# The last o stage by seven block products, and a new order for the second half of a causal attention and squared-ReLU MLP kernel

## The chip, the cores and the metric

The kernel runs on one core of a Trainium2 chip. The metric is device time in microseconds (us) of one execution; the profiled execution is one of its runs, read instruction by instruction. The engines are named as the profile names them: PE is the matrix engine (PEld its weight loads), DVE the vector engine, ACT the scalar engine, POOL the general engine, SP the engine that only issues DMAs (SPq, ACTq and POOLq are the DMA issues of those engines).

## What is computed

```python
# q, k, v: 4 batches x 12 heads x 448 x 64, float32; w_in 768 x 2048, w_out 2048 x 768
scores = scale * q @ k.T                      # per batch and head, causal mask
attn = softmax(scores)
x = (attn @ v).transpose(0, 2, 1, 3).reshape(1792, 768)
h = np.maximum(x @ w_in, 0.0)
out = (h * h) @ w_out
```

## The kernel before, in words

**Products.** Every float32 operand of the MLP is split into a high and a low float32r part, and one product of 128 x 128 by 128 x 448 elements is three matmuls: high by high, high by low, low by high. The MLP works in the transposed sense: tiles of h and of the output have features on the partitions and the 448 tokens of one batch along the row.

**Two halves.** The tokens of batches 0 and 1 (the first half) go through plain products (`h_unit`, `o_unit`), while the attention of the other two batches runs between them. The second half, batches 2 and 3, is worked as a 2 x 2 block scheme: x, w_in and w_out are cut in blocks 11, 12, 21, 22, and sums of blocks (s1 to s4 of the weights, t1 to t4 of the left factors) let seven block products do what eight would do. The stages of the second half take the four groups of 512 hidden features in the order `TURNS = (0, 3, 2, 1)`. `h_pair(gr, u)` makes one half of a group's h (21 products of three matmuls), and `o_seven(gr)` multiplies it with w_out and adds to sums in SBUF (`late["sum"]`, tiles sa and sb) after each product: 7 products x 3 column blocks d x 2 halves u x 3 = 126 matmuls.

**The last o stage.** For the last group, gr = 1, `o_last` works without the seven-product scheme: 4 output blocks x 3 column blocks x 4 products x 3 = 144 matmuls. Each of its 12 output tiles lies in one PSUM bank (tiles ps), is added on DVE to its sum (line 269), transposed on DVE (line 1019) and stored by four DMAs (line 1024, issued by SP or ACT). The last tile, block 22 with d = 2, goes through `finish` instead: two adds, four small transposes on PE (line 1046), copies on ACT and DVE (line 1055), and three DMAs (line 1061).

**Weights.** `w_parts` and `o_parts` bring the weight blocks. Blocks 11, 12 and 22 are loaded ready split by SP (line 944 for w_out, from the DRAM tensor wo_split; line 783 for w_in). The sums s1 to s4 come from `added_up`: SP loads two whole blocks (line 718), POOL issues DMAs that add further blocks onto them in SBUF (line 725), ACT or POOL copies (line 735), and `split` makes the high part (line 266 on ACT, line 279 on POOL) and the low part (line 269 on DVE or 273 on POOL). The last o stage before takes four direct loads a half and no `added_up`. A finished weight block lies in one of nine slots of kind "w": eight pieces of the tile wi, and w3. The slot of a block is taken up again once the last matmul that reads it is through.

**The order.** No scheduler runs. Every operation of the plan has a code in the table `PLACES`: sorting by it gives the order of issue, and the code modulo 3 says which of the offered engines does it. Each engine works through its own operations in that order, and semaphores hold an instruction until its operands are there and its buffer is free. Banks and slots are handed out in this order too.

The lines of the profile that the prediction uses: 843, 845, 847 (matmuls of `h_pair`), 969 to 971 (matmuls of both o stages), 266 (any ACT copy or function), 269 (any two-operand DVE operation), 273 (the same on POOL), 279 and 735 (POOL copies).

## Time and profile before

| | |
|---|---|
| median of 3 runs (lowest to highest) | 601.54 us (601.0 to 602.06) |
| the profiled execution, its own time | 601.9 us |
| its span, first to last instruction | 599.8 us |
| outside the span | 2.1 us |
| PE busy | 582.2 us, 97% |
| DVE, ACT, POOL busy | 454.8, 351.7, 274.5 us |
| the chain that ended last: share of PE | 91% |

The page shows one execution. Busy times of an engine overlap with those of others; the chain that ended last tells what the end waited for, step by step back from the last instruction. A matmul's own duration in the trace (0.36 us) is longer than the distance to the next one's start (0.20 us), since matmuls are pipelined: what a matmul costs the engine is that distance.

### The profile page before, as it was taken

The page shows a single profiled execution, that of the slowest core. Times are in us where ns is not written, and L with a number is a line of the kernel's source. Part 1 is how long each engine was busy: PE and PEld are TensorE (multiplying, and loading weights), DVE is VectorE, ACT ScalarE, POOL GpSimd, SP SyncE. Part 2 cuts the span into 40 slices and gives each one's busy share as a digit, 9 for nine tenths or more (in the row PEclk, how much of TensorE's full clock was granted, in tenths as well). Part 3 has the DMA queues.
Part 4 walks back from the last instruction along what each step waited for, and adds up shares of the span by engine and source line. Part 5 has one row for each costly group of instructions (what it writes and reads, how often), then busy time and mean ns, then how long its engine had stood idle before and what let it go on. Part 6 is the DMA issues. An engine that isn't in the chain of part 4 may idle for free.

```text
span 599.8 us, 11359 instructions
## 1 busy us (share of the span) xinstructions
PE 582.2 (97%) x3718; PEld 510.0 (85%) x3718; DVE 454.8 (76%) x1077; ACT 351.7 (59%) x893; POOL 274.5 (46%) x378
## 2 busy tenths in 40 slices
PE   3899999999999999999999999999999999999997
PEld 2577778798988998988889889999999999999996
DVE  5999998688966898897798658577638758776674
ACT  3899987776756853767457442247565645633310
POOL 2566652243135352333224453654766566756310
PEclk9899999999999999999999999999999999999999
DMA  8888534999888987995899699867877766773556
GB/s 148 188 174 203 141 65 111 259 275 315 225 249 248 267 221 171 298 288 154 222 294 309 219 294 277 252 195 175 234 159 172 149 142 144 168 174 60 162 97 103
DMA packets 190650, 119.99 MB, mean 200 GB/s; under 512 B 126016, under 2 KB 178560, under 8 KB 190592
## 3 DMA queue, kind: packets, MB, share of 16 engines
q1 hardware_dynamic: 169488, 107.99, 64.4%
q0 software_dynamic: 6912, 9.44, 10.2%
q10 hardware_dynamic: 14192, 1.85, 1.9%
q8 instruction: 29, 0.48, 0.4%
q14 instruction: 29, 0.24, 0.1%
HBM read 80.71 MB, written 38.54 MB: 199 GB/s over the span
## 4 chain that ended last, share of the span: by engine, by line
PE 91%; ACT 3%; DMA 3%; DVE 1%; SPq 1%; issue 0%; POOL 0%; ACTq 0%
PE ps L1081 7%; PE ps L662 7%; PE ps L1083 7%; PE ps L1082 7%; PE ps L464 6%; PE ps L663 6%; PE ps L664 6%; PE ps L847 6%; PE ps L845 6%; PE ps L843 6%; PE ps L971 6%; PE ps L969 6%; PE ps L970 6%; PE ps L422 6%; PE ps L380 5%; ACT bp L397 1%
## 5 line engine op out<-in xcount | busy, mean ns | idle before, releaser
L266 ACT ACTIVATE words<-words 128x384 f32<-128x384 f32 (+3 forms) x128 | 73.6, 596 | 35.1 <-DVE words L269 11.4
L1081 PE MATMUL ps<-wo,g 128*128 128x384 f32 x224 | 77.3, 345 | 0.0
L393 DVE CUSTOM_DVE_ANT_0 ps<-ps,mask 128x64 f32<-128x64 f32 (+6 forms) x168 | 68.0, 444 | 11.1 <-PE ps L380 9.7
L1083 PE MATMUL ps<-wo,g 128*128 128x384 f32 x224 | 75.1, 335 | 0.0
L1082 PE MATMUL ps<-wo,g 128*128 128x384 f32 x224 | 75.1, 335 | 0.0
L397 ACT ACTIVATE ap<-ps,mx 128x256 f32<-128x256 f32 (+6 forms) x126 | 58.8, 479 | 26.4 <-DVE mx L393 25.5
L662 PE MATMUL ps<-x,wi 128*128 128x448 f32 x192 | 73.7, 384 | 0.0
L663 PE MATMUL ps<-x,wi 128*128 128x448 f32 x192 | 70.2, 365 | 0.0
L664 PE MATMUL ps<-x,wi 128*128 128x448 f32 x192 | 70.2, 365 | 0.0
L406 POOL TENSOR_SCALAR ap<-ap,asm 128x256 f32<-128x256 f32 (+6 forms) x80 | 43.0, 555 | 46.1 <-DVE asm L499 20.6
L970 PE MATMUL ps<-g,wi 128*128 128x448 f32 x153 | 56.0, 366 | 0.0
L971 PE MATMUL ps<-g,wi 128*128 128x448 f32 x153 | 56.0, 366 | 0.0
L969 PE MATMUL ps<-g,wi 128*128 128x448 f32 x153 | 56.0, 366 | 0.0
L273 POOL TENSOR_TENSOR wi<-words,wi 128x384 fp32r<-128x384 f32 (+1 forms) x38 | 45.7, 1227 | 21.4 <-ACT wi L266 20.6
L845 PE MATMUL ps<-x,wi 128*128 128x448 f32 x150 | 55.0, 367 | 0.0
L847 PE MATMUL ps<-x,wi 128*128 128x448 f32 x150 | 55.0, 367 | 0.0
L843 PE MATMUL ps<-x,wi 128*128 128x448 f32 x150 | 54.9, 366 | 0.0
L266 ACT ACTIVATE r<-ps 128x448 f32<-128x448 f32 x56 | 30.1, 542 | 35.5 <-PE ps L847 18.1
L269 DVE TENSOR_TENSOR g<-r,g 128x448 fp32r<-128x448 f32 x54 | 37.4, 703 | 11.1 <-ACT g L266 7.0
L266 ACT ACTIVATE r<-r 128x448 f32<-128x448 f32 x58 | 32.9, 574 | 17.8 <-DVE r L269 17.1
L1081 PEld LDWEIGHTS ps<-wo,g 128*128 128x128 f32 x224 | 42.1, 188 | 1.0 <-issue 0.4
L266 ACT ACTIVATE wi<-words 128x384 fp32r<-128x384 f32 (+1 forms) x53 | 28.5, 545 | 24.6 <-PE ps L970 8.5
(158 smaller groups left out, 1470.4 us busy)
## 6 DMA issues: line engine op xcount, KB each, us to landing
words<-in_moe_w_in_dram SPq DMA_DIRECT2D x24, 512.0 KB, 5.5
words<-in_moe_w_out_dram SPq DMA_DIRECT2D x32, 384.0 KB, 3.8
wo_split<-wo SPq DMA_DIRECT2D x26, 384.0 KB, 4.5
wi<-wo_split SPq DMA_DIRECT2D x22, 384.0 KB, 3.6
wo_whole<-words SPq DMA_DIRECT2D x32, 192.0 KB, 3.5
wi_split<-wi SPq DMA_DIRECT2D x24, 256.0 KB, 3.7
v<-in_v_dram SPq DMA_DIRECT2D x24, 192.0 KB, 4.0
wi_whole<-words SPq DMA_DIRECT2D x18, 256.0 KB, 4.0
```

The source lines that it names most:

```text
L266: return (ACT, t_act(n, psum, more), lambda: nc.scalar.activation(dst(), src(), func, **kw))
L662: nc.tensor.matmul(o, w[:, 0], x[:, 0], start=c == 0, stop=False)
L663: nc.tensor.matmul(o, w[:, 0], x[:, 1], start=False, stop=False)
L664: nc.tensor.matmul(o, w[:, 1], x[:, 0], start=False, stop=c == NP - 1)
L845: nc.tensor.matmul(o, w.t[:, 0, c], x[:, 1], start=False, stop=False, skip_group_check=True)
L847: nc.tensor.matmul(o, w.t[:, 1, c], x[:, 0], start=False, stop=c == CB - 1, skip_group_check=True)
L969: nc.tensor.matmul(o, w.t[:, 0, d], g.t[:, 0], start=start, stop=False, skip_group_check=True)
L970: nc.tensor.matmul(o, w.t[:, 0, d], g.t[:, 1], start=False, stop=False, skip_group_check=True)
L971: nc.tensor.matmul(o, w.t[:, 1, d], g.t[:, 0], start=False, stop=stop, skip_group_check=True)
L1081: nc.tensor.matmul(res(), g[:, 0], w[:, 0], start=f == 0, stop=False)
L1082: nc.tensor.matmul(res(), g[:, 0], w[:, 1], start=False, stop=False)
L1083: nc.tensor.matmul(res(), g[:, 1], w[:, 0], start=False, stop=f == GF - 1)
```

## The change

The last o stage goes by seven products too. `o_last` now loops over the column blocks d outermost, and within a d over the seven products of `O_LAST`, which says for each product its bank and the sum that it is added to: 7 x 3 x 2 x 3 = 126 matmuls. The products 11, 12, s1 open a bank; s2 and 12 go on in another product's bank, so that a bank is added to a sum on DVE more than once while it fills. `put_out` holds the transposes and stores, and the last tile, which goes through `finish`, is block 21 with d = 2. The last `h_pair`'s four results are no longer only split: they are combined by three subtractions into t1 to t4 and split like the other groups'. The last group's w_out blocks come by three direct loads a half and by `added_up`. The buffers of x (tiles x_t and x2_) are handed on once the last `h_pair` has read them, as slots of kind "g7" (factors) and "w" (weights). The stages of the end change places: (1,0), (1,1), o of group 2, o of group 1, where before o of group 2 stood between (1,0) and (1,1). Two stores to wo_split fall away.

```diff
+    lent_x = dict(zip(
+        [(key, i) for key in ("11", "21", "t3", "t1", "t2", "t4", "22") for i in range(CB)],
+        plan.lend("g7", [lambda i=i: x7[("11", "21", "t3")[i // CB], i % CB]() for i in range(3 * CB)])
+        + plan.lend("w", [...])))
...
-            if (a % 2, ch) != (0, 1) or gr == TURNS[-1]:
+            if (a % 2, ch) != (0, 1):
...
-    def h_pair(gr, u, W, rank, step, plain):
+    def h_pair(gr, u, W, rank, step):
...
-        if plain:
-            factor("12", "12", True)
-            return rank
         less("11", "12", "11")
         factor("t1", "11", True)
...
+    O_LAST = {"11": ("a", "11"), "12": ("b", "11"), "s2": ("a", "12"), "s1": ("c", "22"),
+              "s3": ("a", "22"), "s4": ("c", "12"), "22": ("a", "21")}
...
-        for m, key in enumerate(("11", "12", "22") if gr != TURNS[-1] else ("11", "12", "21", "22")):
+        for m, key in enumerate(("11", "12", "22")):
...
-            if gr != TURNS[-1]:
-                added_up(rank, CH, source, done, lambda t: t, True)
+            added_up(rank, CH, source, done, lambda t: t, True)
...
-        for k in ("11", "21", "12", "22"):
-            i, j = k
-            for d in range(CB):
-                ps, a = Hold("ps", "os"), o_sum(k, d)
-                rank = o_product(ps, [(W[i + m, u], g7[TURNS[-1], m + j, u]) for m in "12" for u in range(2)],
-                                 d, True, True, rank, step)
-                if (k, d) == ("22", CB - 1):
-                    finish(ps, a, d, rank)
+        bank = {}
+        for d in range(CB):
+            for key, (b, k) in O_LAST.items():
+                begin = key in ("11", "12", "s1")
+                if begin:
+                    bank[b] = Hold("ps", "os")
+                ps, a = bank[b], o_sum(k, d)
+                rank = o_product(ps, [(W[key, u], g7[TURNS[-1], OTHER[key], u]) for u in range(2)],
+                                 d, begin, True, rank, step)
+                if (key, d) == ("22", CB - 1):
+                    finish(ps, k, d, rank)
                     continue
...
+                plan.op(rank, [on_dve(S, a, lambda ps=ps: ps.t[:, :S], a, ALU.add)], [ps], [("sum", k, d)],
+                        drop=[ps] if key in ("12", "22", "s4") else [])
+                if key in ("12", "22", "s3", "s4"):
+                    put_out(k, d, rank)
...
-        stages += [(a, 0) for a in after] + [(gr, None)] + [(a, 1) for a in after]
+        early_pair = after == TURNS[-1:]
+        stages += [(a, 0) for a in after] + [(a, 1) for a in after if early_pair]
+        stages += [(gr, None)] + [(a, 1) for a in after if not early_pair]
...
+            if all(v is None for _, v in stages[n + 1:]):
+                for key, ops in used.items():
+                    over(ops, [lent_x[key, i] for i in range(CB)])
```

The table `PLACES` is another one for the second half. On PE the two programs have the same order up to about 1150 matmuls before the end. 18 matmuls of 448 columns are gone, and nothing else changes in PE's number of instructions. Over the whole program DVE gets 16 two-operand operations of 448 elements more and one of 384 less; ACT gets 28 copies or functions more; POOL gets 16 two-operand operations more, 8 copies less and 8 accumulating DMAs (line 725) more; SP issues 24 direct w_out loads instead of 26, 28 loads of line 718 instead of 24, and 24 stores to wo_split instead of 26.

Where the order differs, at the places that are spoken of below (all line numbers of the program after are some five to fifteen higher; tile names are followed by a buffer number). **SP**, some 165 us before the last matmul: the loads of split blocks of w_out (`wi<-wo_split`) and w_in (`wi<-wi_split`) into slots of wi, before:

```order
L783 DMA wi_91<-wi_split 128x768 [waits DMAHW3_49,PE_49]
L783 DMA wi_91<-wi_split 128x768 [waits DMAHW4_49,PE_49]
L718 DMA words_96<-wi_whole 128x384 [waits DMAHW5_49,DMASW2_49,DVE_49]
L718 DMA words_96<-wi_whole 128x384 [waits DMAHW6_49,DMASW3_49,DVE_49]
L783 DMA wi_91<-wi_split 128x768 [waits DMAHW7_49,DMAHW3_49,PE_49]
L944 DMA wi_91<-wo_split 128x768 [waits DMAHW0_49,PE_49]
L944 DMA wi_91<-wo_split 128x768 [waits DMAHW1_49,DVE_49,PE_49]
L944 DMA w3_4300<-wo_split 128x768 [waits DMAHW2_49,DVE_49,PE_49]
```

and after:

```order
L788 DMA wi_91<-wi_split 128x768 [waits DMAHW4_49,PE_49]
L788 DMA wi_91<-wi_split 128x768 [waits DMAHW5_49,PE_49,Pool_49]
L949 DMA wi_91<-wo_split 128x768 [waits DMAHW6_49,PE_49]
L949 DMA wi_91<-wo_split 128x768 [waits DMAHW7_49,PE_49]
L949 DMA wi_91<-wo_split 128x768 [waits DMAHW6_49,DMAHW0_49,PE_49]
L949 DMA wi_91<-wo_split 128x768 [waits DMAHW1_49,DVE_49,PE_49]
L949 DMA wi_91<-wo_split 128x768 [waits DMAHW4_49,DMAHW2_49,PE_49]
```

The sixth row of after (it waits for DVE too) is the load whose slot is freed on PE by a matmul of line 852, `ps5_118<-x11_90,wi_91`, and which the matmul `ps1_114<-g3_1_4339,wi_91` of line 973 reads 22 rows of PE later; in the program before no slot is refilled in fewer than 28 rows.

**PE**, some 48 us before the end of after, where a bank (ps4) is emptied by ACT between two products; the nearest such place before (ps2, at 558.44 us of the trace):

```order
L847 MATMUL ps2_115<-x2_8_3924,wi_91 128x448
L843 MATMUL ps7_120<-x2_81,wi_91 128x448
L845 MATMUL ps7_120<-x2_81,wi_91 128x448
L847 MATMUL ps7_120<-x2_81,wi_91 128x448
L843 MATMUL ps3_116<-x4_83,wi_91 128x448
L845 MATMUL ps3_116<-x4_83,wi_91 128x448
L847 MATMUL ps3_116<-x4_83,wi_91 128x448
L843 MATMUL ps2_115<-x6_85,wi_91 128x448 [waits Activation_49]
```

and after:

```order
L852 MATMUL ps4_117<-x2_5_3921,wi_91 128x448
L848 MATMUL ps1_114<-x8_87,wi_91 128x448
L850 MATMUL ps1_114<-x8_87,wi_91 128x448
L852 MATMUL ps1_114<-x8_87,wi_91 128x448
L973 MATMUL ps4_117<-g3_95,w3_4342 128x448 [waits Activation_49]
```

Between the matmul that completes the bank and the one that waits for ACT there are six matmuls before and three after.

**DVE**, some 35 us before the end. Before:

```order
L269 TENSOR_TENSOR g2_94<-r2_99,g2_94 128x448
L269 TENSOR_TENSOR g2_94<-r5_102,g2_94 128x448 [waits Activation_49]
L269 TENSOR_TENSOR sb6_4316<-sb6_4316,sa0_3925 128x448
L269 TENSOR_TENSOR g0_92<-f3_0_4301,g0_92 128x448 [waits Activation_49]
L269 TENSOR_TENSOR sb7_4317<-ps1_114,sb7_4317 128x448 [waits PE_49,Pool_49]
L269 TENSOR_TENSOR sb6_4316<-ps5_118,sb6_4316 128x448 [waits DVE_49,PE_49]
L1019 STREAM_TRANSPOSE words_96<-sb6_4316 128x448 [waits DVE_49]
```

and after:

```order
L274 TENSOR_TENSOR sb3_4355<-ps7_120,sb3_4355 128x448 [waits PE_49]
L274 TENSOR_TENSOR x2_0_3916<-r5_102,x2_0_3916 128x448 [waits Activation_49]
L274 TENSOR_TENSOR x2_5_3921<-f3_2_4345,x2_5_3921 128x448 [waits Pool_49]
L274 TENSOR_TENSOR g3_0_4338<-r4_101,g3_0_4338 128x448
L274 TENSOR_TENSOR sb1_4353<-ps3_116,sb1_4353 128x448 [waits PE_49]
L274 TENSOR_TENSOR sb0_4352<-ps4_117,sb0_4352 128x448 [waits DVE_49]
L274 TENSOR_TENSOR sb3_4355<-sb3_4355,sa0_3925 128x448 [waits DVE_49]
```

The last factors (x2 and g tiles that had been x's and g's buffers) are made between adds from PSUM banks of the o stages. Counted in the order, the last 198 matmuls (two stretches of 99) have beside them on DVE 14 two-operand operations on SBUF alone, 36 adds from PSUM and 11 transposes, where before had 13, 21 and 11; and on POOL 18 two-operand operations, where before had 6.

**DVE**, the last rows. Before:

```order
L269 TENSOR_TENSOR sb10_4320<-ps3_116,sb10_4320 128x448 [waits PE_49]
L1019 STREAM_TRANSPOSE words_96<-sb10_4320 128x448 [waits DVE_49]
L269 TENSOR_TENSOR sb11_4321<-ps0_113,sb11_4321 128x192 [waits PE_49,Pool_49]
L269 TENSOR_TENSOR sb11_4321<-ps0_113,sb11_4321 128x256
L1055 COPY words_96<-ps6_119 128x128 [waits DMAHW5_49,DMAHW2_49,DMAHW6_49,DMAHW1_49,PE_49]
```

and after:

```order
L1034 STREAM_TRANSPOSE words_96<-sb11_4363 128x448 [waits DVE_49,Activation_49]
L274 TENSOR_TENSOR sb8_4360<-ps2_115,sb8_4360 128x448 [waits PE_49]
L274 TENSOR_TENSOR sb5_4357<-ps4_117,sb5_4357 128x448 [waits PE_49]
L1034 STREAM_TRANSPOSE words_96<-sb5_4357 128x448 [waits DMAHW6_49,DMAHW5_49,DMAHW7_49,DMAHW0_49,DVE_49]
L274 TENSOR_TENSOR sb8_4360<-ps6_119,sb8_4360 128x256 [waits PE_49,Pool_49]
L274 TENSOR_TENSOR sb8_4360<-ps6_119,sb8_4360 128x192
```

Before, one add and one transpose stand between two tiles' ends; after, the last tile (sb8) is added to twice, with another tile's add and transpose between, and a POOL addition onto it (sb8 with sa2) stands between its two adds. The bank ps2 of its first add is completed nine matmuls before the last one.

## Rows read from the trace of the kernel before

**Rows 1.** The page: busy time, 40 slices, chain.
```profile
span 599.8 us, 11359 instructions
PE 582.2 (97%) x3718; PEld 510.0 (85%) x3718; DVE 454.8 (76%) x1077; ACT 351.7 (59%) x893; POOL 274.5 (46%) x378
...
PE   3899999999999999999999999999999999999997
...
PEclk9899999999999999999999999999999999999999
...
PE 91%; ACT 3%; DMA 3%; DVE 1%; SPq 1%; issue 0%; POOL 0%; ACTq 0%
```
**Rows 2.** Windows of 20 us: busy us (instructions) by engine, clock, DMA share, GB/s.
```profile
360.00:380.00 20.00, 20.00 (x114) 19.79 (x114) 16.80 (x32) 6.39 (x12) 9.86 (x13) 1.00 0.92 277
...
420.00:440.00 20.00, 20.00 (x99) 18.20 (x98) 12.08 (x18) 12.53 (x26) 15.17 (x20) 1.00 0.77 198
...
540.00:560.00 20.00, 20.00 (x99) 18.38 (x99) 14.42 (x23) 7.44 (x16) 10.73 (x14) 1.00 0.32 80
560.00:580.00 20.00, 20.00 (x101) 18.53 (x100) 13.30 (x22) 6.02 (x12) 6.31 (x7) 1.00 0.52 132
580.00:600.00 20.00, 15.44 (x77) 13.63 (x75) 9.85 (x18) 0.38 (x1) 2.27 (x2) 0.93 0.62 105
```
**Rows 3.** PE's waits: line waited for, us in total, times, longest.
```profile
PE ps L380 <- DVE aqt L351: 7.4, 1, 7.4
...
PE ps L1046 <- DVE sb L269: 0.5, 1, 0.5
```
**Rows 4.** Timeline of PE, last o stage, 44 starts apart: start, us, instruction.
```profile
585.39 0.37 PE L969 MATMUL ps<-g,wi 128*128 128x448 f32 x1
585.60 0.36 PE L970 MATMUL ps<-g,wi 128*128 128x448 f32 x1
...
594.31 0.36 PE L971 MATMUL ps<-g,wi 128*128 128x448 f32 x1
```
**Rows 5.** Timeline of all engines, the tail.
```profile
593.80 1.52 ACTq L1024 DMA_DIRECT2D out_dram<-words  x3
...
594.78 0.69 DVE L269 TENSOR_TENSOR sb<-ps,sb 128x192 f32<-128x192 f32 x2 [1.19 <-PE ps L971]
595.19 0.77 PE L1046 MATMUL ps<-ident,sb 128*128 128x128 f32 x4 [0.52 <-DVE sb L269]
...
596.04 0.38 ACT L266 ACTIVATE words<-ps 128x256 f32<-128x256 f32 x1 [20.74 <-DMA out_dram<-words]
596.46 0.42 ACTq L1061 DMA_DIRECT2D out_dram<-words  x1
```
**Rows 6.** Line 944, the direct loads: landing of all 26.
```profile
DMA to landing us min/median/max: 2.8/3.7/5.3
```
**Rows 7.** Timeline around the tightest refill: freeing matmul, SP's load, first reader.
```profile
472.80 0.37 PE L847 MATMUL ps<-x,wi 128*128 128x448 f32 x1
473.20 0.32 SPq L944 DMA_DIRECT2D wi<-wo_split  x1
478.53 0.37 PE L969 MATMUL ps<-g,wi 128*128 128x448 f32 x1
```
**Rows 8.** Timeline of PE and ACT: a bank emptied by ACT for another product.
```profile
558.44 0.37 PE L847 MATMUL ps<-x,wi 128*128 128x448 f32 x1
558.85 0.55 ACT L266 ACTIVATE r<-ps 128x448 f32<-128x448 f32 x1 [3.41 <-PE ps L847]
559.86 0.36 PE L843 MATMUL ps<-x,wi 128*128 128x448 f32 x1
```
**Rows 9.** Groups by line and shape, 360:600, on DVE and POOL: count, busy, mean ns.
```profile
L269 DVE TENSOR_TENSOR sb<-ps,sb 128x448 f32<-128x448 f32 x44 | 26.3, 619 | 18.6 <-PE ps L971 17.9 <-ACT sa L266 0.4
L269 DVE TENSOR_TENSOR g<-r,g 128x448 fp32r<-128x448 f32 x36 | 25.1, 707 | 8.1 <-POOL g L279 4.1 <-ACT g L266 4.0
L269 DVE TENSOR_TENSOR g<-f,g 128x448 fp32r<-128x448 f32 x15 | 12.3, 817 | 2.3 <-ACT g L266 1.7 <-POOL g L279 0.5
L273 POOL TENSOR_TENSOR sb<-sb,sa 128x448 f32<-128x448 f32 x5 | 6.1, 1228 | 11.8 <-DVE sb L269 11.8
```
**Rows 10.** Timeline of DVE and POOL, 450 to 453 us, then of DVE alone.
```profile
450.29 0.81 POOL L279 TENSOR_SCALAR g<-f 128x448 fp32r<-128x448 f32 x1 [1.93 <-DVE f L269]
450.58 0.98 DVE L269 TENSOR_TENSOR g<-r,g 128x448 fp32r<-128x448 f32 x1
451.06 1.39 POOL L273 TENSOR_TENSOR wi<-words,wi 128x384 fp32r<-128x384 f32 x1
451.49 1.45 DVE L269 TENSOR_TENSOR g<-f,g 128x448 fp32r<-128x448 f32 x1
...
565.11 0.61 DVE L269 TENSOR_TENSOR r<-ps,r 128x448 f32<-128x448 f32 x1
565.65 0.61 DVE L269 TENSOR_TENSOR g<-r,g 128x448 fp32r<-128x448 f32 x1
...
573.63 1.17 DVE L1019 STREAM_TRANSPOSE words<-sb 128x448 f32<-128x448 f32 x2
...
587.42 0.62 DVE L269 TENSOR_TENSOR sb<-ps,sb 128x448 f32<-128x448 f32 x1 [1.06 <-PE ps L971]
588.08 0.65 DVE L1019 STREAM_TRANSPOSE words<-sb 128x448 f32<-128x448 f32 x1
```

More of the change, by code (lines that the diff above doesn't have):

```diff
@@ L848, in go @@
                                      skip_group_check=True)
-                plan.op(rank, [(PE, 3 * t_mm(S), go)],
-                        [(w, 0), (w, 1)] + [(("x7", OTHER[key], c), i) for i in range(2)], [ps],
-                        take=ps if begin and c == 0 else None, drop=[w])
+                used.setdefault(OTHER[key], []).append(plan.op(
+                    rank, [(PE, 3 * t_mm(S), go)],
+                    [(w, 0), (w, 1)] + [(("x7", OTHER[key], c), i) for i in range(2)], [ps],
+                    take=ps if begin and c == 0 else None, drop=[w]))
                 rank += step
@@ L929, in o_parts @@
     def o_parts(gr, rank, last):
-        W, Z, gate = {}, {}, list(ahead)
+        W, Z, gate, order = {}, {}, list(ahead), tuple(O_LAST) if gr == TURNS[-1] else SEVEN
         def at(key, u):
-            return rank + (last - rank) * (SEVEN.index(key) + u / 2) / 7
+            return rank + (last - rank) * (order.index(key) + u / 2) / 7
         def flat(t):
@@ new lines, in o_last, with put_out, go @@
+        return rank
+    def put_out(k, d, rank):
+        i, j = k
+        a, h = o_sum(k, d), Hold("f", "tr")
+        plan.op(rank, [(DVE, t_dve(S) + 0.05, lambda: nc.vector.transpose(h.t, a()))],
+                [("sum", k, d)], [h], take=h)
+        row, col = T + (int(j) - 1) * S, (int(i) - 1) * CH + d * P
+        for s in range(P // SQ):
+            def go(eng, s=s):
+                return lambda: eng.dma_start(
+                    out=out[row:row + S, col + s * SQ:col + (s + 1) * SQ].rearrange(
+                        "(b p) d -> p b d", p=SQ),
+                    in_=h.t[s * SQ:(s + 1) * SQ].rearrange("p (b d) -> p b d", d=SQ))
+            plan.op(rank, [(DMA, 0.6, go(nc.sync), t_dma(S, 128)), (DMA2, 0.6, go(nc.scalar), t_dma(S, 128))], [h], [], drop=[h])
@@ L1035, in finish @@
+    def finish(ps, k, d, rank):
+        i, j = k
+        a, row, col = o_sum(k, d), T + (int(j) - 1) * S, (int(i) - 1) * CH + d * P
         for first, end in ((0, 2 * P), (2 * P, S)):
@@ L1046, in turn @@
                     nc.tensor.transpose(turned.t[:n, m - first:m - first + P], a()[:, m:m + n], late["ident"])
-            plan.op(rank, [(PE, 0.22, turn)], [("sum", "22", d, first)], [turned], take=turned)
+            plan.op(rank, [(PE, 0.22, turn)], [("sum", k, d, first)], [turned], take=turned)
             blocks = [(0, 2, P)] if first == 0 else [(0, 1, P), (1, 1, S - 3 * P)]
```

218 lines of the change are left out of this document (104 added, 114 removed).

## The prediction

> **What bounds the kernel now.** I read the page first: PE is busy 97% of the span, from the third slice to the last but one each shows 9 tenths, and PE has 91% of the chain that ended last [rows 1]. Then windows of 20 us: in the second half PE is busy 20.00 of 20 us up to 580 us at a granted clock of 1.00 (2.4 GHz, the upper of its two levels), while DVE, ACT and POOL stay below 17 us [rows 2]. Then PE's waits: the longest are at the start (7.4 us), and the last listed that lies in the second half is the tail's 0.5 us [rows 3]. So matmuls set the time, one after the other without a gap, and a change is worth what it takes out of that row of matmuls, less the waits that it puts in.
>
> **What a matmul is worth.** Its row says 0.36 to 0.37 us, but the next one starts 0.20 us later: from 585.39 to 594.31 there are 44 starts, 0.203 us each [rows 4]. By its own duration a removed matmul would be priced almost twice too high. The Trainium skill, "TensorE: Matmul & The Clock Gate", section "Back-to-back issue gap", gives about 131 ns for sustained matmuls of 512 columns; by that figure 18 matmuls would give 2.4 us, an estimate. This trace, with 0.203 us for 448 columns, does not agree with it, and the trace is used.
>
> **The change part by part.** The sum is made against the profiled execution, 601.9 us (span 599.8 and 2.1 outside); the median of the runs is 0.36 us lower, 601.54, and every difference below is taken from that.
>
> (a) *Removed:* 144 matmuls become 126. 18 x 0.203 = **-3.65 us**, wholly on the path. Nothing else falls off PE, and the first half stays as it is.
>
> (b) *The tail.* Before, the last matmul starts at 594.31, DVE adds from 594.78, ACT copies at 596.04 and its store is issued at 596.46 [rows 4, 5]. After, DVE has another tile's add and transpose to do just ahead of the last adds. The first add onto the last tile can start 0.47 us (594.31 to 594.78) after the bank's last matmul, which is nine starts before the end, so 1.83 - 0.47 = 1.36 us before the last matmul starts; a POOL addition onto the same tile follows it (1.23 us, [rows 9]), and the final add can begin some 0.55 to 0.65 us after the last matmul instead of 0.47. On ACT's queue stand stores of the tile that was just transposed, 0.5 us each (three took 1.52 [rows 5]): three of them after a transpose that ends at +0.6 reach +2.1, where ACT's copy was at +1.73 before. **+0.4**, between 0.1 (stores done earlier) and 0.9 (one store more in the way).
>
> (c) *A slot refilled in a hurry.* Some 160 us before the end a slot of wi is freed by a matmul, refilled by SP from wo_split, and read 22 matmuls later: 22 x 0.203 = 4.47 us. Before, the tightest such place is 28 starts, 5.73 us, from 472.80 to 478.53, with SP's issue 0.40 us after the freeing matmul's start [rows 7]. Landing takes 2.8 to 5.3 us, median 3.7 [rows 6]: 0.40 + 3.7 = 4.1 just fits, 0.40 + 5.3 = 5.7 is late by 1.2. That stretch, 420 to 440 us, has a DMA share of 0.77 and busy engines [rows 2], so I take a landing of 4.5 and **+0.4**, between 0 and 1.2. What stands behind a late load on SP's queue is other loads with more room.
>
> (d) Two more slots are refilled in 25 matmuls, 5.08 us, some 105 and 61 us before the end. With the median they fit by 1.0, with the longest landing each is late by 0.6: **+0.1**, between 0 and 1.2 for both.
>
> (e) *ACT empties a bank while three matmuls run.* At 558.44 a bank's last matmul starts, ACT copies it from 558.85 to 559.40, and the next user starts at 559.86, seven starts later, without waiting [rows 8]. After, at two places (some 125 and 48 us before the end) the next user comes four starts, 0.81 us, later: 0.41 + 0.55 + about 0.05 to hand over is 1.01. 0.2 each, **+0.4**, between 0 and 0.6.
>
> (f) *DVE in the last 40 us.* There the new scheme puts its work: the last factors' low parts, an add for each product instead of one for each tile, and the transposes. I count in the order, for the last 198 matmuls (40.2 us), 14 two-operand operations on SBUF, 36 adds from PSUM and 11 transposes. Back to back, DVE starts an operation 0.54 us after the one before (565.11 and 565.65), and a transpose 0.66 us after the add that it needs (587.42 and 588.08) [rows 10]; the SBUF ones I price at the mean of 0.707 and 0.817 us [rows 9], since they lie beside POOL. 25 x 0.54 + 11 x 0.66 + 11 x 0.585 (1.17 for two in a row [rows 10]) + 14 x 0.76 = 13.5 + 7.3 + 6.4 + 10.6 = 37.8 us, 94% of the stretch. By the same prices before has 21 adds and 13 SBUF operations, 29 us or 72%, which the windows bear out [rows 2]. At 94% an engine that must hand back banks and factors in time falls behind now and then; each delay that reaches PE is of the order of one operation, 0.6 us. Between 0 (all hidden, since sums and transposes can lag a little) and 5 (below), I take **+1.1**, two such delays; a third of this stands for the dense DVE stretch some 70 to 100 us before the end.
>
> What else moves is hidden: 28 more ACT operations at some 0.55 us are 15 us over 230, and ACT was busy 12.5 of 20 us in its fuller windows [rows 2]; two stores to wo_split fewer stood behind no wait.
>
> Sum: -3.65 + 0.4 + 0.4 + 0.1 + 0.4 + 1.1 = **-1.25**: 600.65 for a run like the profiled one, **600.3 us** for the median.
>
> **The rivals.** *A, nothing waits.* The refills land at the median, ACT's hand-over is hidden and DVE's lag is taken up by free banks: -3.65 + 0.4 = 3.25 less, **598.3**, or 598.7 with (e). For it: before has no wait at all in the second half although its DVE windows reach 14 us and more. Against it: the four places of (c) to (e) are tighter than any place that the trace shows to be free of waits.
>
> *B, the refills and hand-overs take it all.* Terms (c) and (d) at their upper ends (1.2 and 1.2), the others as taken: -3.65 + 0.4 + 2.4 + 0.4 + 1.1 = +0.65, **602.2**, no change. It needs the longest landing of 26 three times, so it is unlikely.
>
> *C, slower: DVE becomes the bound of the last 40 us.* At 451.49 an operation g<-f,g took 1.45 us beside a POOL two-operand operation of 1.39 us, at 450.58 another took 0.98 [rows 10], while the 44 adds from PSUM keep 0.619 us [rows 9]. POOL has 18 two-operand operations in this stretch, where it had 6, and DVE 14 that can be hit. If each hit costs 1.45 - 0.76 = 0.69 us, DVE's 37.8 us pass the 40.2 at three and a half hits; with ten it has 44.7 us to do, PE waits 4.5 us in place of 1.1, and the time is 600.3 + 3.4 = **603.7**. It is slower than before by more than the bound below from about nine hits on. For it: the counts, and that the factors so delayed are what PE reads next. Against it: in the whole second half the mean of such operations is only 0.1 to 0.2 us over the undisturbed ones, so most of them miss POOL. The Trainium skill, "SBUF — State Buffer", section "SBUF: two separate sides", states such a rule: a DVE operation with two SBUF inputs and a GpSimd operation that reads SBUF share a pair of ports as an exclusive lock, and the later one waits for the whole of the other. The 1.45 us agrees with it, and so does the unchanged 0.619 us of the adds with one PSUM input; by it, this rival's hits are what is to be expected wherever the two meet.
>
> *D, the change does less than it says.* The order shows 18 matmuls fewer on PE, so the gain (a) can't fail to be there; only an unseen wait in the moved stages could hide it, and then the time is about the old one.
>
> **How the numbers follow.** A measurement of this kernel can tell about 0.2%, 1.2 us, from no change: faster means below 600.3, slower above 602.7. My forecast (600.3, own range 599.2 to 601.5) has 0.47, and since it lies on the bound, 0.26 of this is faster and 0.21 the same. A has 0.25, faster. B has 0.09, the same but for 0.02 slower. C has 0.16, slower. D has 0.03, the same. Together: faster 0.51, same 0.31, slower 0.18. The range takes in A's 598.3 and reaches into C up to 603.0; left out are most of C and the little below 598.3.
>
> **What would show it.** (a) PE's last o stage with 126 matmuls, starts 0.20 us apart between waits. (c), (d): PE waits on a DMA wi<-wo_split at two or three places. (e): two PE waits on ACT of 0.2 us. (f): PE waits on DVE sb or on x2 and g factors in the last 40 us, DVE busy over 18 us in the windows there, and g<-f,g or g<-r,g with a mean near or over 0.8 us. (b): ACT's last copy some 2.1 us after the last matmul's start instead of 1.7. The prediction is wrong if PE waits as little as before in the second half (then it is A), or if DVE's windows at the end are full and PE's below 19 us (then it is C).

## The result, and the profile after

The changed kernel takes **607.81 us** (median of 4 runs, 606.65 to 610.0) against 601.57 us for the kernel before beside it (4 runs): a ratio of 1.0109, 95% interval 1.0094 to 1.0124 (ratios here are taken over the runs, so they are not quite those of the two medians). It is 6.2 us slower, where the prediction had 600.3 us, with the range ending at 603.0. The profiled execution has 607.57 us and a span of 605.8 us.

The page after, with the lines that answer to [rows 1]:

```profile
PE 581.1 (96%) x3700; PEld 506.7 (84%) x3700; DVE 473.5 (78%) x1092; ACT 362.8 (60%) x921; POOL 293.6 (48%) x394
...
PE   3799999999999999999999999999999999999886
...
PEclk9999999999999999999999999999999999999899
...
PE 82%; DVE 7%; DMA 4%; ACT 3%; issue 2%; POOL 0%; SPq 0%; POOLq 0%; DVEq 0%; ACTq 0%
```

PE has the 18 matmuls fewer (3700 for 3718), but its share of the chain fell from 91% to 82%, DVE's rose from 1% to 7%, and PE's slices and its clock have a dent just ahead of the end. The waits of PE in the second half, answering to [rows 3], where only the tail's wait stood (line waited for, us in total, times, longest):

```profile
PE ps L973 <- DVE sb L274: 4.6, 2, 3.0
PE ps L973 <- DMA wi<-wo_split: 1.4, 2, 1.0
PE ps L1061 <- DVE sb L274: 0.6, 1, 0.6
```

And two windows of 20 us, as in [rows 2]:

```profile
540.00:560.00 20.00, 19.98 (x99) 18.13 (x98) 18.70 (x28) 11.20 (x24) 14.99 (x17) 1.00 0.87 211
560.00:580.00 20.00, 15.45 (x67) 13.46 (x67) 17.86 (x20) 4.80 (x11) 11.85 (x12) 0.91 0.38 88
```

From 560 to 580 us PE is busy 15.45 of 20 us, at a mean granted clock of 0.91. The timeline of PE there:

```profile
565.10 0.37 PE L975 MATMUL ps<-g,wi 128*128 128x448 f32 x1
568.46 0.47 PE L973 MATMUL ps<-g,x 128*128 128x448 f32 x1 [2.99 <-DVE sb L274]
...
569.22 0.57 PE L973 MATMUL ps<-g,x 128*128 128x448 f32 x1
569.59 0.57 PE L974 MATMUL ps<-g,x 128*128 128x448 f32 x1
...
576.64 0.37 PE L975 MATMUL ps<-x,x 128*128 128x448 f32 x1
578.57 0.44 PE L973 MATMUL ps<-x,x 128*128 128x448 f32 x1 [1.56 <-DVE sb L274]
```

There are two holes of 3.16 and 1.72 us beyond the usual 0.203, and after the first of them nine matmuls (569.22 to 572.55) start 0.37 us apart, at nearly half the rate: PE had stood idle, and the granted clock fell to 0.50 (1.2 GHz, the lower of its two levels) for 3.3 us. That is another 1.5 us. What DVE did meanwhile, from its timeline (start, duration, operation):

```profile
562.14 3.20 DVE L274 TENSOR_TENSOR sb<-sb,sa 128x448 f32<-128x448 f32 x1
565.27 2.60 DVE L274 TENSOR_TENSOR g<-r,g 128x448 fp32r<-128x448 f32 x1
567.79 1.14 DVE L274 TENSOR_TENSOR sb<-ps,sb 128x448 f32<-128x448 f32 x2
...
573.29 2.99 DVE L274 TENSOR_TENSOR x<-r,x 128x448 fp32r<-128x448 f32 x1
```

POOL in the same stretch:

```profile
561.69 0.88 POOL L730 DMA_DIRECT2D words<-wo_whole  x1
562.29 2.29 POOL L278 TENSOR_TENSOR x<-words,x 128x384 fp32r<-128x384 f32 x2
564.23 1.18 POOL L730 DMA_DIRECT2D words<-wo_whole  x1
564.83 1.60 POOL L278 TENSOR_TENSOR wi<-words,wi 128x384 fp32r<-128x384 f32 x1
566.16 1.22 POOL L278 TENSOR_TENSOR wi<-f,wi 128x384 fp32r<-128x384 f32 x1
...
571.68 0.86 POOL L730 DMA_DIRECT2D words<-wo_whole  x1
572.29 1.30 POOL L278 TENSOR_TENSOR wi<-words,wi 128x384 fp32r<-128x384 f32 x1
573.25 2.54 POOL L278 TENSOR_TENSOR sb<-sb,sa 128x448 f32<-128x448 f32 x2
```

Three DVE operations of 0.61 us took 2.6 to 3.2 us. Each has both inputs in SBUF, and the last two end 0.49 us behind the end of a row of POOL operations that follow each other without a pause (a *train* below): 567.87 behind 567.38, 576.29 behind 575.79. Behind them on DVE's queue stands the add sb<-ps,sb at 567.79 that hands PE its bank; the bank's last matmul had ended at 563.03, and PE had been waiting since 565.3. The adds from PSUM keep 0.61 us, as in [rows 9].

**The account.** Up to the last matmul of the attention PE has the same order in both kernels. From that matmul's start to the end, before took 248.54 us, after takes 254.78, 6.24 more. Excess of each gap between two starts over 0.203: first hole 3.16, second 1.72, half rate 1.5 (term f: 6.4); two waits for loads, 1.20 at 485.88 and 0.53 at 531.31 (d); two places where ACT empties a bank, 0.29 and 0.29 (e); the tail, 5.91 us from the last product's start to the end, where it was 5.47 (b: 0.44); and a wait of 0.39 at 358.39, among the last plain products of the first half. Less 3.65 these make +5.9; 0.3 us are not assigned.

### The profile page after: what moved, and what is told of

It is laid out like the page before. It is cut to its first block, busy times and chain, and to the rows that moved or that the text cites. A ratio compares the mean times of both kernels' runs of the same rounds, so it can differ in the third digit from the quotient of the medians.

```text
span 605.8 us, 11405 instructions
## 1 busy us (share of the span) xinstructions
PE 581.1 (96%) x3700; PEld 506.7 (84%) x3700; DVE 473.5 (78%) x1092; ACT 362.8 (60%) x921; POOL 293.6 (48%) x394
## 4 chain that ended last, share of the span: by engine, by line
PE 82%; DVE 7%; DMA 4%; ACT 3%; issue 2%; POOL 0%; SPq 0%; POOLq 0%; DVEq 0%; ACTq 0%
PE ps L1096 6%; PE ps L1098 6%; PE ps L667 6%; PE ps L1097 6%; PE ps L469 6%; PE ps L668 6%; PE ps L669 6%; PE ps L848 5%; PE ps L850 5%; PE ps L852 5%; PE ps L427 5%; PE ps L385 5%; PE ps L973 4%; PE ps L975 4%; PE ps L974 4%
## 5 line engine op out<-in xcount | busy, mean ns | idle before, releaser
L271 ACT ACTIVATE words<-words 128x384 f32<-128x384 f32 (+3 forms) x139 | 79.5, 590 | 47.8 <-DVE words L274 12.3
L667 PE MATMUL ps<-x,wi 128*128 128x448 f32 x192 | 73.7, 384 | 0.0
L668 PE MATMUL ps<-x,wi 128*128 128x448 f32 x192 | 70.2, 366 | 0.0
L669 PE MATMUL ps<-x,wi 128*128 128x448 f32 x192 | 70.2, 365 | 0.0
L848 PE MATMUL ps<-x,wi 128*128 128x448 f32 x156 | 57.2, 367 | 0.1
L850 PE MATMUL ps<-x,wi 128*128 128x448 f32 x156 | 57.2, 367 | 0.0
L852 PE MATMUL ps<-x,wi 128*128 128x448 f32 x156 | 57.2, 366 | 0.0
L278 POOL TENSOR_TENSOR wi<-words,wi 128x384 fp32r<-128x384 f32 (+1 forms) x39 | 47.4, 1219 | 18.3 <-ACT wi L271 17.5
L271 ACT ACTIVATE wi<-words 128x384 fp32r<-128x384 f32 (+1 forms) x58 | 30.9, 540 | 37.0 <-PE ps L850 11.4
L274 DVE TENSOR_TENSOR g<-r,g 128x448 fp32r<-128x448 f32 x54 | 41.8, 779 | 7.9 <-ACT g L271 7.7
L1096 PEld LDWEIGHTS ps<-wo,g 128*128 128x128 f32 x224 | 42.1, 188 | 1.0 <-issue 0.4
L1098 PEld LDWEIGHTS ps<-wo,g 128*128 128x128 f32 x224 | 42.0, 188 | 0.6 <-DVE g L274 0.6
L1097 PEld LDWEIGHTS ps<-wo,g 128*128 128x128 f32 x224 | 42.1, 188 | 0.4
L274 DVE TENSOR_TENSOR sb<-ps,sb 128x448 f32<-128x448 f32 (+2 forms) x55 | 32.1, 607 | 12.4 <-PE ps L975 11.9
L385 PE MATMUL ps<-akt,aqt 64*64 64x192 f32 (+5 forms) x504 | 33.3, 398 | 8.5 <-DVE aqt L356 7.7
```

The costliest lines, as they stand in the source:

```text
L271: return (ACT, t_act(n, psum, more), lambda: nc.scalar.activation(dst(), src(), func, **kw))
L274: return (DVE, t_dve(n) + more, lambda: nc.vector.tensor_tensor(out=dst(), in0=a(), in1=b(), op=op))
L667: nc.tensor.matmul(o, w[:, 0], x[:, 0], start=c == 0, stop=False)
L668: nc.tensor.matmul(o, w[:, 0], x[:, 1], start=False, stop=False)
L669: nc.tensor.matmul(o, w[:, 1], x[:, 0], start=False, stop=c == NP - 1)
L848: nc.tensor.matmul(o, w.t[:, 0, c], x[:, 0], start=begin and c == 0, stop=False, skip_group_check=True)
```

## The experiments

**1. The ports by themselves.** In a kernel of nothing but DVE and POOL operations, eight of each per stage.

> Leaves out the whole computation; the output is zeros. Seven stretches, each started for DVE and POOL by the same ACT copies, time eight DVE operations of 128x448 beside eight POOL operations of 128x384. My theory (the lock: a DVE operation with two SBUF inputs waits for POOL operations, and for several when they stand back to back): DVE alone starts one every 0.54 us; beside POOL two-operand operations back to back, DVE operations with two SBUF inputs take 1.4 to 3 us each and the eight take 8 us or more; with one input from PSUM they keep 0.54 to 0.62 us; transposes keep 0.6 us. Rival (the long operations of the kernel come from something else: matmuls or DMAs that read the same buffers): all stretches show 0.54 to 0.62 us a DVE operation. What a POOL operation with one input does to DVE is open.

Alone, DVE's eight take 4.30 us and POOL's eight adds 7.67. Together:

```profile
42.37 9.17 DVE L149 TENSOR_TENSOR d<-a,b 128x448 f32<-128x448 f32 x8 [26.57 <-ACT b L166]
58.84 4.34 DVE L152 TENSOR_TENSOR d<-ps,b 128x448 f32<-128x448 f32 x8 [7.30 <-ACT b L166]
70.98 6.21 DVE L149 TENSOR_TENSOR d<-a,b 128x448 f32<-128x448 f32 x8 [7.80 <-ACT b L166]
84.02 4.33 DVE L155 STREAM_TRANSPOSE d<-a 128x448 f32<-128x448 f32 x8 [6.83 <-ACT a L166]
...
43.30 10.05 POOL L158 TENSOR_TENSOR q<-c,e 128x384 f32<-128x384 f32 x8 [4.84 <-ACT e L168]
```

Two inputs in SBUF beside POOL's adds: the two engines strictly alternate, and DVE needs twice its time. One input in PSUM, or a transpose: no effect. POOL operations with a single input (third row) delay DVE too, to 0.78 us each. So there is a lock, but here it costs one POOL operation a time, 1.4 us at most, not 3.

**2. Less work for POOL.** The eight low parts of the last o stage's summed w_out blocks are copied on ACT instead of subtracted on POOL; the subtraction itself is left out. DVE keeps every operation.

```diff
-        plan.op(rank, two_sources(n, lo, src, lambda: hi().bitcast(F32), ALU.subtract)[ways],
+        plan.op(rank, [on_act(n, lo, src)] if low_on_act else
+                two_sources(n, lo, src, lambda: hi().bitcast(F32), ALU.subtract)[ways],
```

> The changed kernel, but the low parts of the last o stage's summed weights (8 POOL two-operand operations of 1.0 to 1.3 us in its last 45 us) are copied on ACT instead of subtracted on POOL: their values are not the low parts. DVE keeps every operation. Theory (the lock makes DVE late): the DVE operations of 2.5 to 3.2 us at the end fall to 0.6 to 1.4 us, PE's two waits on DVE sb (4.6 us) and the half-rate stretch behind them (1.5 us) go for the most part, and the time falls by 4 to 6 us to 602 to 604 us. Rival (DVE has too many operations in the last 40 us, whoever runs beside it): PE still waits 4 us or more on DVE, the time stays within 1.5 us of 607.8.

607.2 us, 1.0106 (1.0076 to 1.0135): nothing gained. The operations at 562 us were short now, but one DVE operation later took 5.52 us, and PE waited 3.1 us for it:

```profile
570.75 5.52 DVE L274 TENSOR_TENSOR sb<-sb,sa 128x448 f32<-128x448 f32 x1
...
569.96 0.86 POOL L731 DMA_DIRECT2D words<-wo_whole  x1 [6.91 <-ACT words L271]
570.52 3.70 POOL L278 TENSOR_TENSOR sb<-sb,sa 128x448 f32<-128x448 f32 x3
573.88 0.82 POOL L284 TENSOR_SCALAR wi<-words 128x384 fp32r<-128x384 f32 x1
574.36 1.43 POOL L278 TENSOR_TENSOR sb<-sb,sa 128x448 f32<-128x448 f32 x1
```

Five POOL operations passed before one DVE operation got in. Fewer POOL operations do not help by themselves; one long hold is enough. Whether DVE simply has too much to do is not settled here, since its work was the same.

**3. Half of each direct load.** The three direct loads per half of w_out bring the high part only and leave out the low part, which those products read too.

```diff
-                    out=w.t.bitcast(F32).rearrange("p i c n -> p i (c n)"), in_=wh_dram[gr, a + GF * ch]), t_dma(2 * P, 4 * CH))],
+                    out=w.t[:, 0].bitcast(F32).rearrange("p c n -> p (c n)"), in_=wh_dram[gr, a + GF * ch][:, 0]), t_dma(2 * P, 4 * CH))],
```

> The changed kernel, but the direct loads of w_out blocks bring the high half only (192 instead of 384 KB each); the low parts are stale. Theory (the two PE waits on a DMA wi<-wo_split, 1.2 and 0.5 us beyond the normal distance, come from slots that are refilled and read within 25 matmuls): landing falls by 0.5 us or more, these two waits shrink to under 0.5 us together, and the time falls by 1 to 2 us to about 606.2 us; the waits on DVE stay. Rival (the waits only move: what PE gains there it waits later for DVE): the two waits go, but the time stays within 0.5 us of 607.8.

604.69 us (603.1 to 606.83), 1.0055 (1.0039 to 1.0071), 3.1 less than the changed kernel. PE's waits for loads fell from 1.4 to 0.4 us in the profile, the waits for DVE stayed (4.7 for 4.6), and the median landing fell from 5.0 to 4.0 us. So the loads are a part, by the profile the smaller one. But the profiled run is the longest of the seven, so what makes up the other 2 of the 3.1 us isn't seen, and by the time alone half loads are worth half of what was lost.

**4. What makes a train hold the ports?** Stages of six POOL operations without a pause, in five forms, and one DVE operation in the middle.

> A kernel that leaves the whole computation out. Eight stages, in each POOL runs six operations on SBUF back to back while DVE does five adds from PSUM, then one or two operations with both inputs in SBUF, then more adds from PSUM. In the stages, in order: POOL adds of 384 columns into another tile; of 448 columns; of 448 columns in place; the same with DVE's operations in place too; POOL subtractions of 384 columns with another output type; DVE's one operation waiting for a late ACT copy; two DVE operations in a row; a one-input POOL operation as fourth of the six. The theory of trains expects DVE's lone operation to last until POOL's six are all done, 2 us and more, in at least one of these forms, and the form tells what holds the ports. The rival, that a DVE operation lets one POOL operation past at most as in the alternation seen before, expects no lone operation above 1.9 us (0.61 plus one POOL operation of at most 1.3) in any stage; then the 3.20 and 5.52 us of the kernel have another cause than the ports.

The rival is borne out: in the stages where the two met, the second, third, sixth and eighth, the lone operation lasted 1.09 to 1.48 us, and the two in a row of the seventh 2.56. The first, fourth and fifth told nothing, since DVE's operation ran when POOL's train was over or not begun. A train alone does not do it. In these stages DVE's operation came during the second or third POOL operation; in 1, at 43.44, one came during the first of eight and lasted 1.42 us.

**5. DVE's adds ahead of the operations that were held.** Only DVE's order is changed.

```diff
 L274 TENSOR_TENSOR sa_3927<-ps_113,sa_3927 128x448
-L274 TENSOR_TENSOR sb_4363<-sb_4363,sa_3927 128x448
-L274 TENSOR_TENSOR g_94<-r_100,g_94 128x448
 L274 TENSOR_TENSOR sb_4362<-ps_118,sb_4362 128x448
 L274 TENSOR_TENSOR sb_4357<-ps_116,sb_4357 128x448
+L274 TENSOR_TENSOR sb_4363<-sb_4363,sa_3927 128x448
```

> The changed kernel with six entries of its order moved on DVE's queue alone, in the last 50 us: the adds that empty PE's banks stand ahead of the three operations that waited out POOL's trains (3.20, 2.60 and 2.99 us), and these stand where their results are first needed; everything else is in the same order. The theory (a locked DVE operation waits out a train, and a bank's add stands behind it) expects the two PE waits of 3.16 and 1.72 us and the nine matmuls at half the clock (1.5 us) to go, though the long DVE operations stay long: some 6.0 us less than the changed kernel's 607.8, 601.5 to 602.5. The rival, that DVE as a whole has too much to do there, expects the wait to move to another DVE result and no more than 1.5 us of gain: 606 or more.

607.83 us, 1.0095 (1.0073 to 1.0117): a miss. The first hole was gone, but g<-r,g now took 4.43 us at 574.42, and PE waited 4.0 us behind it. In this trace, that of the longest of the four runs (609.63 us), PE also waited 2.2 us for a load. Another order on DVE did not end the waits; another operation was caught. But the traces of four kernels (the changed one, 2, 3 and 5) now held 17 DVE operations of 2.5 us and more in the second half, and ahead of each, or in the train that it waited for, stood a **DMA issue on POOL**; trains without one had cost 1.6 us.

**6 and 7. The DMA issue.** In the first of two kernels POOL issued its DMAs too early or too late: no DVE operation on SBUF met the operations behind an issue (the longest lasted 1.55 us), and it decided nothing.

> A kernel that leaves the whole computation out. In the traces of the whole kernels every DVE operation that waited out more than one POOL operation (2.5 to 5.5 us) has a DMA issue on POOL just ahead of, or in, the train that it waited for; a train without one held it for one operation (1.6 us). Seven stages, POOL's train of five in-place adds of 448 columns and DVE's lone operation on SBUF after four adds from PSUM: an accumulating DMA issue ahead of the train; the same behind its second operation; no DMA; an accumulating DMA ahead of five one-input operations; a plain DMA ahead of the train; an accumulating DMA, with DVE's adds all from PSUM; two adds and then three accumulating DMAs. The theory (after a DMA issue POOL keeps the ports until its train ends) expects DVE's lone operation to last until the end of the train in the first, second and perhaps fifth stage, 3 to 5 us, about 1.1 to 1.5 us in the third, and adds of 0.6 us in the sixth. The rival, that the DMA issue has nothing to do with it, expects about 1.1 to 1.5 us in all of them, as in the stages without a DMA measured before.

The second has the issue beside DVE's work.

> A kernel that leaves the whole computation out; the measurement before, mended so that POOL's DMA issue starts beside DVE's work (its destination is written by ACT just before). Ten stages: a train of five POOL adds with no DMA; an accumulating DMA issue and five adds, with DVE's lone operation on SBUF after one, two, three and four adds from PSUM; one add, the DMA issue, four adds; the DMA issue and five subtractions of 384 columns, with the lone operation after one and two; a plain DMA issue and five adds; two accumulating DMA issues and four adds. The theory (POOL keeps the ports from a DMA issue until its train ends) expects the lone operation to last to the end of the train, 4 to 6 us, in at least the stages where it starts beside the DMA issue. The rival expects no more than 1.6 us in any stage.

POOL and DVE in the third stage (issue and five adds, DVE's operation third), and DVE's in the third to fifth:

```profile
50.44 0.88 POOL L199 DMA_DIRECT2D words<-x_dram  x1 [7.20 <-ACT words L187]
51.05 5.75 POOL L174 TENSOR_TENSOR q<-q,e 128x448 f32<-128x448 f32 x5
...
50.83 6.46 DVE L153 TENSOR_TENSOR d<-a,b 128x448 f32<-128x448 f32 x1
...
70.82 5.91 DVE L153 TENSOR_TENSOR d<-a,b 128x448 f32<-128x448 f32 x1
...
90.19 5.38 DVE L153 TENSOR_TENSOR d<-a,b 128x448 f32<-128x448 f32 x1
```

6.46 us for one DVE operation: it ends at 57.29, 0.49 us behind the whole train (56.80). It also waited for the end of the train when it came while the first POOL operation was already running (70.82, 90.19), and behind a plain DMA issue too (6.18 us) as behind an accumulating one. It took 0.62 us where it came ahead of the issue or between two issues, so the issue itself does not hold it; the operations behind it do. The stage without an issue told nothing, since POOL's train was over before DVE began; the comparison is with 1 and 4. This is the theory, shown at the smallest scale: **POOL operations that follow a DMA issue without a pause keep the ports for their whole train; without the issue, DVE gets in after one of them.**

The traces of the whole kernels set two limits to it. A short pause ends the hold: in the changed kernel POOL pauses for 0.09 us at 435.89, and the DVE operation that began at 433.72 ended 0.49 us behind that point. And the time of arrival counts. Every DVE operation that was held for 2.5 us or more came within 1.8 us of the start of an issue. Three that came 2.3 us or more behind one, in trains without a visible pause, got in after one POOL operation: 1.33 us at 561.42 in 9, and 0.91 and 0.87 us at 563.45 and 562.27 in e11 and e13 (below). No run was made to test what ends the hold there.

**8. The kernel without the DMA issues.** The last o stage's eight accumulating issues are left out, and with them the sums of w_out blocks that they form:

```diff
             plan.op(at, [(POOL, 1.1, lambda: nc.gpsimd.dma_start(
-                out=shaped(h.t[:, :n]), in_=src, accum_op=ALU.add))], saved, [h])
+                out=shaped(h.t[:, :n]), in_=src, accum_op=ALU.add) if sums else None)], saved, [h])
```

> The changed kernel without the eight accumulating DMA issues on POOL that prepare w_out for the last o stage; all other instructions are the same and in the same order, but the sums are then not formed, so what the last stage adds up is not the product. The theory (a POOL DMA issue makes the following train of POOL operations hold the ports until it ends) expects no DVE operation above 1.7 us in the last 60 us, so no PE wait of 3.2 and 1.7 us there and no half clock: 601 to 602.5. The rival, that back-to-back trains alone do it, expects the trains to stay (four and three operations back to back) and with them DVE operations of 2.5 us and more and PE waits of 2 us and more: 605 or more. Since POOL and ACT no longer wait for the sums to land, trains can also shift by a few us under either.

603.17 us (600.86 to 606.19), 1.0027 (1.0008 to 1.0046): 4.6 us less, a little short of what was expected. The train is unbroken now from 562.07 to 572.13, ten us, and DVE's operations beside it:

```profile
563.51 1.44 DVE L274 TENSOR_TENSOR g<-r,g 128x448 fp32r<-128x448 f32 x1
...
565.94 1.35 DVE L274 TENSOR_TENSOR g<-r,g 128x448 fp32r<-128x448 f32 x1
567.21 1.43 DVE L274 TENSOR_TENSOR sb<-sb,sa 128x448 f32<-128x448 f32 x1
...
571.04 1.57 DVE L274 TENSOR_TENSOR x<-f,x 128x448 fp32r<-128x448 f32 x1
```

None above 1.6 us; PE's longest wait for DVE there is 1.1 us, and the half clock is gone. The ACT work that these sums feed no longer waits for them either, and PE's waits for loads fell from 1.4 to 0.2 us beside the missing DMAs, so this alone would not settle it; with 7 and 9 it does.

**9. The same issues, elsewhere.** The whole kernel, with four of POOL's issues moved to where POOL must wait next, and one operation (f<-f,r) given to DVE. POOL's order in the last 50 us:

```diff
-L730 DMA words<-wo_whole 128x384 x2
+L730 DMA words<-wo_whole 128x384 x3
...
-L278 TENSOR_TENSOR f_2_4345<-f_2_4345,r_101 128x448
 L730 DMA words<-wo_whole 128x384
 L278 TENSOR_TENSOR x_80<-words,x_80 128x384
 L278 TENSOR_TENSOR x_79<-words,x_79 128x384
-L730 DMA words<-wo_whole 128x384
```

> The changed kernel, whole, with four of POOL's DMA issues moved in its order to places behind which POOL must wait for another engine (one at the start of the second half, three in the last 50 us), and one two-operand operation that stood between two of them given from POOL to DVE; the rest of the order is as it was. The theory (a POOL DMA issue makes the POOL operations that follow without a pause hold the ports, and DVE's next operation on SBUF waits until they end) expects DVE operations of at most 1.7 us in the last 60 us, no PE wait of 3.2 and 1.7 us, no half clock there: 4 to 6.5 us less than the changed kernel's 607.8, 601.3 to 603.8. The rival (trains of POOL operations hold the ports with or without a DMA issue) expects the same long waits, since the trains are as long as before or longer: 606 or more.

602.53 us (601.5 to 604.59), 1.0020 (1.0009 to 1.0030): 5.3 us less than the changed kernel, with the same work, as the theory had it. Two of its DVE operations are above the 1.7 us expected: 2.68 at 542.58, behind two issues that were not moved, and 2.14 at 557.76, in a train behind two issues (554.55 and 555.08), ending 0.49 us behind the train. PE still waits 1.8 us for loads and 1.6 for DVE.

**10 to 13. Versions meant to be better.** e10 adds DVE's order of 5 and moves six groups of three matmuls ahead of the readers of the two late loads; e11 and e12 mend places where PE still waited; e13 is e12 without one of its moves.

> A repaired version: e9_dma_apart, with DVE's adds that empty PE's banks ahead of the operations that can be held, and with six groups of three matmuls moved ahead of the first readers of the two loads that PE waited for (1.2 and 0.5 us), so that each load has 1.2 to 1.8 us more. By the theory the sum is then the prediction's terms (a), (b) and (e) almost alone, -3.65 + 0.4 + 0.6: some 599 us, 598.5 to 601, faster than the kernel before. By the rival it is no better than e9_dma_apart less the two waits.

602.18 us, 1.0009 (0.9998 to 1.0021): less than hoped. Both waits for loads are gone, but f<-f,r on DVE was caught (2.82 us) and PE waited 1.5 us for an add behind five operations on SBUF.

> e10_repaired with DVE's order mended at the two places where PE still waited for it: the add that PE waited 1.66 us for (behind four operations on SBUF) stands ahead of two of them that are needed only later, and the operation of 2.82 us that had been given to DVE is back on POOL, at the end of its train, with ACT's use of it moved behind. The rest as in e10_repaired. By the theory its profiled execution loses another 1.7 to 2.0 us, to a span of some 597.3, and the median comes to 599.5 to 601.0, faster than the kernel before by a few tenths of a per cent; if the waits merely move on to the next DVE result, it stays at 602.

601.49 us, 0.9996 (0.9987 to 1.0005): level with before, half a us short of what was expected. Its second half is 0.9 us shorter than that of e10 in the profiles (247.74 and 248.66), but its first half, the same instructions, took 1.1 us more: so much two executions can differ.

> e11_repaired2 with four places of DVE's and ACT's order mended where PE still waited 0.3 to 0.4 us each in its profile (an add that hands back a bank ahead of a transpose and two later operands, twice; another add ahead of its neighbour; ACT's copy of a bank ahead of a copy that is needed later). Everything else as in e11_repaired2 (601.5). If these waits were the only rest, 1.0 to 1.5 us less: 600.0 to 600.7, 0.15 to 0.25% faster than the kernel before. If the rest of the gain is lost elsewhere (the first half's own spread, waits that move on), 601.2 to 601.7.

603.70 us, 1.0033 (1.0021 to 1.0045), a miss, and the most telling one. To bring an add forward I had moved the first transpose and its stores back; ACT no longer waited for that transpose, handed POOL its next operand at once, and the last DMA issue lost the pause behind it.

> e11_repaired2 with the four small places of e12_repaired3 mended, but with the first transpose and its stores left where they were in e11_repaired2, so that ACT waits there as before and POOL gets a pause behind its last DMA issue. The theory of the ports expects no DVE operation above 1.7 us there and none of the 2.1 us wait and half clock of e12_repaired3: 600.0 to 600.9, 0.1 to 0.3% faster than the kernel before. If e12_repaired3 lost its time to the moved adds and not to the DMA issue that lost its pause, this one stays at 603.

**600.60 us** (599.49 to 600.97, 11 runs), 0.9981 (0.9972 to 0.9990): faster than the kernel before by 0.2%, the best version here. It has as many instructions on every engine as the changed kernel. The same place in e12 (POOL, then DVE):

```profile
569.91 0.86 POOL L730 DMA_DIRECT2D words<-wo_whole  x1
570.52 1.30 POOL L278 TENSOR_TENSOR wi<-words,wi 128x384 fp32r<-128x384 f32 x1
...
570.38 3.03 DVE L274 TENSOR_TENSOR g<-r,g 128x448 fp32r<-128x448 f32 x1
```

and in e13:

```profile
569.37 0.86 POOL L730 DMA_DIRECT2D words<-wo_whole  x1
575.43 1.01 POOL L278 TENSOR_TENSOR wi<-words,wi 128x384 fp32r<-128x384 f32 x1 [5.21 <-ACT wi L271]
...
569.85 0.61 DVE L274 TENSOR_TENSOR g<-r,g 128x448 fp32r<-128x448 f32 x1
```

The same operation, 0.5 us behind the same DMA issue: 3.03 us where POOL goes on at once, 0.61 where it pauses. In e12 PE waited 2.1 us behind it, and the half rate came back.

## Why the prediction was wrong

**(a) The matmuls, right.** In e13 the only wait of PE that the view lists for the second half is the tail's 0.6 us. From the last matmul of the attention to the end it takes 246.41 us, 2.13 less than before. The sum is -3.65 + 0.45 (tail) + 1.07 (small gaps left) = -2.13: the 18 matmuls are worth their 0.203 us each.

**(b) The tail, right:** 0.44 for +0.4.

**(c) and (d) The refills, mis-sized.** At (c) PE did not wait (0 for 0.4). At (d) it waited 1.20 and 0.53 us, 1.7 for 0.1. The places of (d) were the right ones; the price rested on [rows 6], landing 2.8 to 5.3 us with a median of 3.7. The direct loads of the changed kernel:

```profile
DMA to landing us min/median/max: 2.9/5.0/8.4
```

The two waited for took 5.74 and 5.10 us. The loads of before were no measure for loads in another company; what slows them is not settled.

**(e) ACT's two places, right:** 0.29 at each, for 0.2.

**(f) DVE at the end, the step that failed: 6.4 us for 1.1.** It is rival C's mechanism at another price. The count was fair, but a full DVE by itself costs PE next to nothing: e13 has the same work on DVE, its windows are about as full as those of the changed kernel (18.70 and 17.86 us, there with the waiting inside the long operations), and PE stays at 19.90 us and more:

```profile
540.00:560.00 20.00, 19.97 (x98) 17.86 (x97) 18.90 (x29) 13.84 (x30) 17.57 (x20) 1.00 0.91 206
560.00:580.00 20.00, 19.90 (x98) 17.86 (x97) 17.36 (x30) 2.59 (x6) 14.56 (x14) 1.00 0.46 105
```

What failed is the price of a delay. A hit was priced at 0.69 us, from one pair of operations [rows 10], and "each delay that reaches PE is of the order of one operation". In truth two kinds of hits exist. A plain one costs up to 1 us, as in 1, 4 and 8. One behind a DMA issue costs all that POOL has queued, 2 to 5 us, and so a bank's add comes that much late. The change had raised just this: POOL's DMA issues from 540 us on, in the groups by line (count, busy us, mean ns), before:

```profile
L725 POOL DMA_DIRECT2D words<-wi_whole x2 | 1.8, 880 | 0.0
```

and after:

```profile
L730 POOL DMA_DIRECT2D words<-wo_whole x9 | 9.0, 1027 | 3.2 <-ACT words L271 2.9 <-POOL f L740 0.3
```

Seven products need sums of blocks of w_out, and the sums are made by accumulating DMAs on POOL. I counted POOL's 18 two-operand operations, but not the issues between them, which stood in the same order. The wait also cost something that no term had: the clock's lower level for nine matmuls, 1.5 us.

**The wait at 358.39,** 0.39 us, had no term. It is the same mechanism: a DMA issue at 355.22, two operations without a pause, and words<-words on DVE took 2.45 us.

**The rule on the ports.** The Trainium skill, "SBUF — State Buffer", section "SBUF: two separate sides", says that of a DVE operation with two SBUF inputs and a GpSimd operation that reads SBUF the first to start holds the shared pair for the whole instruction. The runs agree where no DMA issue stands ahead (1.09 us beside adds of 1.14 in 4; alternation in 1). For an operation that comes soon behind an issue they don't: 6.46 us are five instructions, and the measurement decides.

The chances were wrong in the same place. C had 0.16, with "most of them miss POOL" against it, a mean over the whole second half. Where the hits fall, and what stands behind them, was to be read from the two queues side by side.

## What to carry to other kernels

Read a helper engine's queue for what stands *between* its operations: on POOL, a DMA issue that is followed without a pause makes everything behind it one long hold of the ports, and a DVE operation with two SBUF inputs that comes soon after the issue waits it out. Put such an issue where POOL has to wait next (9 and e13). Adds that empty PSUM ahead of DVE's operations on SBUF are part of e10 to e13, but by themselves, in 5, they gained nothing. Issuing these DMAs from another engine was not tried. And an order that fits so tightly must be read again after each move: e12 lost 3 us because ACT had stopped waiting.

## What the runs showed of the hardware

- A DVE operation on two SBUF tiles, 0.61 us alone, lasted 6.46 us behind a POOL DMA issue and five adds, and 5.52 us in a whole kernel; without the issue it stayed below 1.7 us beside trains of up to ten us (8). It ended 0.49 us behind the train. Three that came 2.3 us or more behind the issue were held for one operation only.
- POOL operations with a single input delay DVE as well (eight in 6.21 us for 4.30); adds with one input in PSUM (4.34) and transposes (4.33) are not touched.
- After PE waits of 3.0, 3.1 and 4.0 us the next matmuls ran at half rate, 0.37 us apart, for about 3 us; after waits of 1.5 and 1.6 us they did not, and of four waits of 2.1 to 2.4 us two were followed by it. This can make a wait cost half as much again.
